# Moving the first part of a memory update from slot 8 to slot 9 of each segment's plan

## The chip, the cores and the metric

The kernel runs on one core of a Trainium2 chip. The metric is the device time of one execution in microseconds; less is better. TensorE (PE) multiplies, VectorE (DVE) and ScalarE (ACT) take results out of PSUM and do elementwise work, GpSimd (POOL) masks and adds in SBUF, SyncE (SP) issues nearly all DMAs.

## The reference

One layer over 2048 rows of width 640 in bf16. The rows are normalised and go through an attention with a compressive memory (32 heads of 20, 4 segments of 512 rows) and, separately, through a gated unit of width 1536; the output joins the two.

```python
xn = _layernorm(x)
for s in range(N):                      # 4 segments of L = 512
    p = softmax(einsum('bhqd,bhkd->bhqk', qs, ks) * scale + mask)
    a_dot = einsum('bhqk,bhkd->bhqd', p, vs)
    a_mem = einsum(phi(qs), M) / (einsum(phi(qs), z) + 1e-06)
    o = g * a_mem + (1.0 - g) * a_dot
    M = M + einsum('bhld,bhle->bhde', phi(ks), vs)
    z = z + einsum('bhld->bhd', phi(ks))
s = o @ wo
out = x + s * silu((sigmoid(xn @ w_gate) * (xn @ w_up)) @ w_down)
```

Here `phi(t)` is `t + 1` where `t > 0` and `exp(t)` elsewhere. The memory `M, z` that segment n leaves is read in segment n + 1.

## The kernel before

Every engine's work is issued in an order written out by the program; each engine runs its own queue in that order, and a wait holds what stands behind it. A segment is 20 slots (`NSLOT`), one pass over the heads in 4 pairs of head groups, five slots `u` = 0 to 4 for each pair (`UNITS`). A head group is 4 heads.

In a slot (the loop from L716) the program issues in this order:

- `scores` (L516): score matmuls `Sps` into four PSUM banks, of which there is one set only; then the exponential `pt` on ScalarE (L527, 128x2048) and the causal select on GpSimd (L530). The next slot's scores need the exponential done.
- an early part: tasks of the plan due before `now + 0.45`, and filler.
- `weigh` (L534) of the slot before: matmuls `Aps` of `pt` with the values, into a PSUM bank of which there is one. A head group ends with `u` = 2 for the first group and `u` = 4 for the second; then VectorE makes rd, rd and od (L553, L554, L556), and od frees that bank. The weighting of slot `u` runs in slot `u + 1`, so a head group ends in slots whose place in the pair is 3 (slots 3, 8, 13, 18) and 0.
- a late part: tasks due before `now + 1.0`, and filler.

All other matmuls write into a ring of three PSUM banks (`dtile`, tag "d"). Which of the three a new tile gets follows from the order in which earlier tiles were released in the program, so it is not strictly the oldest; TensorE then waits for the engine that reads that bank out. In the early part (`delay[0]`) k and v results are taken out by VectorE, otherwise by ScalarE.

The tasks have a due time in slots and a cost (`at`, L103). For the following segment: v tiles (`psv`, L360), k and q chunks (`psk` L289, `psq` L321), the q bound (`cps`, L334, copied out as `cb` and relayed through DRAM into QT); for the segment before: the o-projection (`sp`, L502, out as `aa`) and the output; for the segment itself the memory read (`mem_read`: matmuls `am` L410, then rm L415, rm L417 and om L418 on VectorE, om freeing the bank) and the memory update.

The memory update, `m_update` (L381), is issued in two parts: chunks 0 to 2 and chunks 3 and 4 of the 640 rows of `M`. The first part is 12 matmuls `dm` (L388) into one bank of the ring, then three VectorE products with a block mask. In segment 0 these write `Mbd` (L396). In segments 1 and 2 they write `dmb` (L399), of which there are two buffers, and GpSimd adds each into `Mbd` (L400). Segment 3 has none.

The filler is the gated unit: `gate` (`gp`, L428, five matmuls, then tg on ScalarE), `up` (L438, five matmuls, then hT on VectorE) and `down` (`yp`, L456, twelve matmuls). Before each segment the planner adds up what each slot already has, `fixed`, from a table of the weighting and the costs of the tasks due in it, and finds a common `level`; each slot's share of filler is what it lacks of that level. Shares add up in `goal`, and a filler group is issued when at least half its cost is covered:

```python
        fixed = [PASS[i % NU] + sum(t[2] for t in tasks if i <= t[0] - NSLOT * n < i + 1) for i in range(NSLOT)]
        level = min(fixed)
        while sum(max(level - f, 0.0) for f in fixed) < left:
            level += 0.01
```

Of the kernel before, what the change touches and what calls it, by code (L numbers as in the profile page):

```python
# [55 lines left out]
R = NSLOT / 24  # L56
# [3 lines left out]
def kernel(  # L60
# [42 lines left out]
    def at(time, cost, fn, *a):  # L103
        count[0] += 1
        heapq.heappush(first if fn is phi else tasks if cost > 0.1 else soft, (time, count[0], cost, fn, a))
# [533 lines left out]
    for n in range(NSEG):  # L639
        w = NSLOT * n  # L640
        m = n + 1
        if m < NSEG:
            if n:
                for p in range(2):
                    for i in range(2):
                        at(w + (-1.4, -0.7, 0.1, 0.55)[2 * p + i], 0.1, ln_stats, m, p, i, i + 1)
                        at(w + (0.6, 0.9, 1.7, 2.0)[2 * p + i], 0.1, ln_norm, m, p, i)
            for i in range(8):
                at(w + R * (3.5 + (0.6 * i if i < 4 else 2.5 + 0.55 * (i - 4))), 0.68, v_tile, m, i // 2, i % 2)
            for c in range(DC):  # L650
                at(w + R * (8.8 + 1.0 * c if n else 9.4 + 0.9 * c), 1.08, k_chunk, m, c)
                at(w + R * (13.8 + 1.1 * c), 1.08, q_chunk, m, c)
                if m + 1 < NSEG:
                    at(w + R * (12.8 + 0.85 * c), 0.0, phi, m, "k5", c)
                at(w + R * (17.4 + 0.8 * c), 0.0, phi, m, "q5", c)
            at(w + R * 19.2, 0.6, q_bound, m)
            if m + 1 < NSEG:
                for p in range(2):
                    at(w + R * (16.1 + p), 0.0, x_load, m + 1, p)
            if n == 0:  # L660
                for c in range(DC):
                    at(R * (2.6 + 0.8 * c), 0.0, phi, 0, "k5", c)
            for i, cs in enumerate(([0, 1, 2], [3, 4])):
                at(w + R * (10.0 + 3.2 * i), 0.75 - 0.25 * i, m_update, n, cs)
        if n >= 1:
            for j in range(4):
                at(w + R * (1.1 + 0.3 * j), 0.0, o_ready, n - 1, j)
                at(w + R * (4.0 + 0.5 * j if j < 3 else 9.6), 0.0, xr_load, n - 1, j)
            for i in range(8):
                at(w + R * (5.4 + 1.1 * i), 0.68, o_proj, n - 1, i // 2, i % 2)  # L670
                at(w + R * (3.4 + 0.85 * i), 0.25, mem_read, n, i // 2, i % 2)
# [74 lines left out]
    n = NSEG - 1  # L746
# [39 lines left out]
```

## Time and profile before

| | us |
|---|---|
| median of 3 runs | 338.39 |
| lowest, highest run | 338.29, 341.84 |
| profiled execution, its own time | 339.99 |
| its span, first to last instruction | 338.3 |

The page names an instruction group by line, engine and operation, with the tiles it writes and reads (out<-in). A row of the timeline has start, length, engine, line, operation, tiles, shapes and count; brackets at its end hold the engine's idle time just before it and the instruction whose end released it. A row of the chain of waits has start, length and the engine and tile on which the time depended. A row of waits has the total in us, the number of waits and the longest. Slots begin at the `Sps` rows: slot 8 of segment 0 at 60.53 us, of segment 1 at 134.23, of segment 2 at 213.47.

### The profile page before, as it was taken

To read this page: it belongs to the slowest core of one execution; us is meant where nothing else is said; L and a number is where in the kernel's file an instruction comes from. 1 tells how busy PE (TensorE), PEld (TensorE's weight loads), DVE (VectorE), ACT (ScalarE), POOL (GpSimd) and SP (SyncE) were. 2 spreads that over 40 slices of the span, in tenths; PEclk is the share of its full clock that TensorE was granted. 3 is DMA by queue.
4 is the path that set the end of the run, shared out by engine and by line. 5 is a ranking of instruction groups with operands and counts; after the bars stand their busy time and mean duration, and the time that the engine had idled before them with its cause. 6 is when DMAs were issued, how large, how long until landed. Compare 5 with 4: busy or idle time off the path is not lost.

```text
span 338.3 us, 8318 instructions
## 1 busy us (share of the span) xinstructions
PE 326.1 (96%) x3360; PEld 186.5 (55%) x3402; DVE 223.9 (66%) x532; ACT 226.5 (67%) x237; POOL 111.0 (33%) x157
## 2 busy tenths in 40 slices
PE   8999899999999999999999999999999999999995
PEld 7544455445665565554566466554456655544673
DVE  6375356479877577778775977876673687533355
ACT  3653797778786666477876765565887776786730
POOL 6645232232325322332223622333222323233214
PEclk9999999999999999999999999999999999999999
DMA  7956994774840731045730263042220521210032
GB/s 237 343 183 194 265 112 83 234 214 91 186 109 3 131 92 53 20 137 88 203 94 2 54 105 98 21 155 86 74 70 3 83 76 41 63 55 3 2 62 78
DMA packets 54725, 35.53 MB, mean 105 GB/s; under 512 B 28576, under 2 KB 54688, under 8 KB 54688
## 3 DMA queue, kind: packets, MB, share of 16 engines
q1 hardware_dynamic: 52480, 32.23, 37.7%
q10 hardware_dynamic: 2208, 2.79, 2.7%
q8 instruction: 26, 0.43, 0.6%
q14 instruction: 11, 0.09, 0.1%
HBM read 20.19 MB, written 8.39 MB: 84 GB/s over the span
## 4 chain that ended last, share of the span: by engine, by line
PE 87%; DMA 5%; DVE 3%; ACT 2%; issue 1%; POOL 0%; SPq 0%; DVEq 0%; ACTq 0%; POOLq 0%
PE yp L456 14%; PE up L438 14%; PE gp L428 13%; PE Aps L547 9%; PE Sps L522 7%; PE sp L502 6%; PE psk L289 6%; PE psq L321 6%; PE psv L360 6%; DMA Wu<-in_B_w_up_dram 2%; PE wps L571 2%; DMA xnT<-xn 1%; PE dm L388 1%; PE am L410 1%; ACT pt L527 1%
## 5 line engine op out<-in xcount | busy, mean ns | idle before, releaser
L527 ACT ACTIVATE pt<-Sps 128x2048 bf16<-128x2048 f32 x80 | 150.1, 1876 | 24.6 <-PE Sps L522 21.3
L530 POOL TENSOR_SCALAR_AFFINE_SELECT pt<-pt 128x1024 bf16<-128x1024 bf16 (+1 forms) x80 | 76.4, 956 | 197.8 <-ACT pt L527 197.8
L438 PE MATMUL up<-xnT,Wu 128*128 128x512 bf16 x229 | 58.8, 379 | 1.5 <-DVE Mbd L396 0.7
L428 PE MATMUL gp<-xnT,Wg 128*128 128x512 bf16 x221 | 58.0, 379 | 2.1 <-DMA Wg<-in_B_w_gate_dram 0.9
L456 PE MATMUL yp<-Wd,hT 128*128 128x320 bf16 x384 | 57.1, 299 | 0.0
L442 DVE SCALAR_TENSOR_TENSOR hT<-tg,up 128x512 bf16<-128x512 bf16 x48 | 32.7, 681 | 32.1 <-PE up L438 29.2
L431 ACT ACTIVATE tg<-gp 128x512 bf16<-128x512 f32 x48 | 28.6, 597 | 35.4 <-PE gp L428 34.7
L547 PEld LDWEIGHTS <-pt 128*128 128x128 bf16 x1280 | 43.1, 96 | 14.7 <-DVE od L556 2.1
L547 PE MATMUL Aps<-va,pt 128*128 128x21 bf16 x1280 | 44.5, 173 | 0.9 <-DVE od L556 0.8
L456 PEld LDWEIGHTS <-hT 128*128 128x128 bf16 x384 | 35.4, 97 | 15.7 <-issue 2.8
L438 PEld LDWEIGHTS <-Wu 128*128 128x128 bf16 x240 | 21.4, 97 | 24.4 <-issue 3.1
L428 PEld LDWEIGHTS <-Wg 128*128 128x128 bf16 x240 | 20.9, 97 | 22.6 <-issue 1.7
L461 DVE SCALAR_TENSOR_TENSOR aa<-t,yp 128x320 bf16<-128x320 bf16 x32 | 15.4, 482 | 26.7 <-ACT t L459 26.5
L522 PE MATMUL Sps<-QT,KT 24*128 24x128 bf16 (+3 forms) x512 | 32.0, 301 | 0.8 <-ACT pt L527 0.4
L360 PE MATMUL psv<-Wv,xnT 128*128 128x320 bf16 x160 | 26.4, 299 | 0.2
L459 ACT ACTIVATE t<-yp 128x320 bf16<-128x320 f32 x32 | 14.0, 437 | 18.4 <-PE yp L456 17.2
L502 PE MATMUL sp<-Wo,oT 128*128 128x320 bf16 x160 | 25.9, 300 | 0.0
L321 PE MATMUL psq<-xnT,Wq 128*128 128x512 bf16 x96 | 23.6, 380 | 0.6 <-issue 0.5
L289 PE MATMUL psk<-xnT,Wk 128*128 128x512 bf16 x92 | 23.5, 379 | 0.5 <-issue 0.2
L522 PEld LDWEIGHTS <-KT 24*128 24x128 bf16 x512 | 9.3, 92 | 25.5 <-issue 23.9
L504 DVE SCALAR_TENSOR_TENSOR aa<-aa,sp 128x320 bf16<-128x320 bf16 x32 | 15.5, 484 | 9.5 <-PE sp L502 9.5
L502 PEld LDWEIGHTS <-oT 128*128 128x128 bf16 x160 | 14.5, 98 | 8.0 <-issue 2.0
(74 smaller groups left out, 327.3 us busy)
## 6 DMA issues: line engine op xcount, KB each, us to landing
KT<-Ks SPq DMA_DIRECT2D x32, 80.0 KB
QT<-Qs SPq DMA_DIRECT2D x32, 80.0 KB
xr<-in_A_x_dram SPq DMA_DIRECT2D x15, 160.0 KB
out_dram<-xr SPq DMA_DIRECT2D x15, 160.0 KB
xt<-in_A_x_dram SPq DMA_DIRECT2D x6, 320.0 KB
Wg<-in_B_w_gate_dram SPq DMA_DIRECT2D x3, 640.0 KB
Wu<-in_B_w_up_dram SPq DMA_DIRECT2D x3, 640.0 KB
Wd<-in_B_w_down_dram ACTq DMA_DIRECT2D x1, 1920.0 KB
```

The lines of the kernel that those rows point to most:

```text
L289: nc.tensor.matmul(ps[:], lhsT=W["k"][:, k, c * P:(c + 1) * P], rhs=s["xnT"][:, k, :], start=(k == 0), stop=(k == DC - 1))
L321: nc.tensor.matmul(ps[:], lhsT=W["q"][:, k, c * P:(c + 1) * P], rhs=s["xnT"][:, k, :], start=(k == 0), stop=(k == DC - 1))
L360: nc.tensor.matmul(ps[:], lhsT=s["xnT"][:, k, j * P:(j + 1) * P], rhs=W["v"][:, k, half * HB:(half + 1) * HB], start=(k == 0), stop=(k == ...
L428: nc.tensor.matmul(gp[:], lhsT=Wg[f // 4][:, k, fo:fo + P], rhs=s["xnT"][:, k, :], start=(k == 0), stop=(k == DC - 1))
L438: nc.tensor.matmul(ps[:], lhsT=Wu[f // 4][:, k, fo:fo + P], rhs=s["xnT"][:, k, :], start=(k == 0), stop=(k == DC - 1))
L442: empty(lambda: nc.vector.scalar_tensor_tensor(out=h[:], in0=tg[:], scalar=1.0, in1=ps[:], op0=ALU.add, op1=ALU.mult))
L456: nc.tensor.matmul(yp[:], lhsT=s["hT"][f][:, j * P:(j + 1) * P], rhs=W["d"][:, f, hs], start=(f == 0), stop=(f == FC - 1))
L502: nc.tensor.matmul(sp[:], lhsT=s["oT"][:, j, c, :], rhs=W["o"][:, c, hs], start=(c == 0), stop=(c == DC - 1))
L522: nc.tensor.matmul(Sps[:, r, c0:c0 + ncol], lhsT=kt[32 * r:32 * r + KR, gi, kb * P:(kb + 1) * P], rhs=qt[32 * r:32 * r + KR, gi, kb * P:L] ...
L527: nc.scalar.activation(pt[:], Sps[:], ACT.Exp, scale=SCALE)
L530: nc.gpsimd.affine_select(out=diag, in_=diag, compare_op=ALU.is_ge, fill=0.0, base=0, pattern=[[0, 4], [0, cnt], [1, P]], channel_multipli ...
L547: nc.tensor.matmul(A[:, qb, r, :], lhsT=pt[:, r, off:off + P], rhs=V[4 * (n % 2) + kb][:, 4 * g + r, :], start=first, stop=True, skip_grou ...
```

## The change

The first part's due time becomes 9.05 slots in every segment instead of `R * 10.0`, which is 8.33 with `R` = 20/24. The second part keeps 11.0. Costs stay 0.75 and 0.5. At 8.33 the first part falls into the early part of slot 8 (place 3 of its pair), at 9.05 into that of slot 9 (place 4). In segments 1 and 2 it then stands behind the k chunk due at 9.0; in segment 0 ahead of the one due at 9.33. As its cost leaves one slot of `fixed` for the next, the planner's shares change too.

```diff
-                at(w + R * (10.0 + 3.2 * i), 0.75 - 0.25 * i, m_update, n, cs)
+                at(w + (9.05, 11.0)[i], 0.75 - 0.25 * i, m_update, n, cs)
```

## The prediction

> **What bounds the kernel now.** I read the page's busy shares and its chain of waits first, then TensorE's waits, then the timeline around the moved step in each of the three segments that have it.
>
> ```profile
> span 338.3 us, 8318 instructions
> ...
> PE 326.1 (96%) x3360; PEld 186.5 (55%) x3402; DVE 223.9 (66%) x532; ACT 226.5 (67%) x237; POOL 111.0 (33%) x157
> ...
> PEclk9999999999999999999999999999999999999999
> ...
> PE 87%; DMA 5%; DVE 3%; ACT 2%; issue 1%; POOL 0%; SPq 0%; DVEq 0%; ACTq 0%; POOLq 0%
> ```
> TensorE is busy 326.1 of 338.3 us at its full clock and makes 87% of the chain. The same matmuls run after the change, so only TensorE's idle time can go or come. It has names:
>
> ```profile
> PE Aps L547 <- DVE od L556: 0.8, 2, 0.4
> PE up L438 <- DVE Mbd L396: 0.7, 1, 0.7
> ...
> PE Sps L522 <- ACT pt L527: 0.4, 1, 0.4
> ```
> The 0.7 and half of the 0.8 lie at the moved step. In segment 0, slot 8:
>
> ```profile
> 60.53 0.39 PE L522 MATMUL Sps<-QT,KT 24*128 24x512 bf16 x4
> ...
> 60.85 0.98 PE L388 MATMUL dm<-va,pkt 128*128 128x147 bf16 x12
> 61.67 0.35 PE L547 MATMUL Aps<-va,pt 128*128 128x21 bf16 x8
> ...
> 61.87 0.77 DVE L396 TENSOR_TENSOR Mbd<-dm,BD 128x147 bf16<-128x147 f32 x3 [3.48 <-PE dm L388]
> ...
> 62.69 1.24 PE L438 MATMUL up<-xnT,Wu 128*128 128x512 bf16 x5 [0.67 <-DVE Mbd L396]
> ```
> The `up` group was given the PSUM bank that dm had just used, so it waits until VectorE's three products are out: 0.67 us. In segment 1 the chain of waits itself leaves TensorE at this place:
>
> ```profile
> 137.57 0.82 PE dm L388 x12
> ...
> 138.41 0.33 DVE dmb L399
> ...
> 138.81 0.48 POOL Mbd L400
> ...
> 139.31 0.33 DVE dmb L399
> ...
> 140.65 0.50 DVE od L556
> ...
> 141.19 0.76 PE Aps L547 x24
> ```
> ```profile
> 141.19 0.76 PE L547 MATMUL Aps<-va,pt 128*128 128x21 bf16 x24 [0.43 <-DVE od L556]
> ```
> dm's three products, the third of them held by GpSimd's add (two dmb buffers), stand on VectorE ahead of the pass that ends the head group; od empties the only Aps bank late, and slot 9's 24 weighting matmuls idle 0.43 us. Segment 2 has the same order, but its `Aps` row carries no idle time:
>
> ```profile
> 219.85 0.75 PE L547 MATMUL Aps<-va,pt 128*128 128x21 bf16 x24
> ```
>
> **What the change removes.** The dm group (12 matmuls with their weight loads, no DMA) starts after slot 9's scores instead of slot 8's, so slot 8's rd, rd and od no longer have the products before them. Slot 9 ends no head group. In segment 0 the built order gives slot 8 `up`, Aps, `gate`, k and slot 9 dm, k, Aps x24; in segments 1 and 2 slot 9 is k, dm, o-projection, Aps x24, k. No `up` follows dm into its bank. Removed: 0.67 + 0.43 + 0 = 1.10 us.
>
> What is late next at these places: in segment 0, slot 9 loses a `gate` group and becomes the shortest stretch that an exponential must fit into.
>
> ```profile
> 64.94 0.40 PE L522 MATMUL Sps<-QT,KT 24*128 24x128 bf16 x8
> ...
> 65.53 1.88 ACT L527 ACTIVATE pt<-Sps 128x2048 bf16<-128x2048 f32 x1
> ...
> 66.36 0.75 PE L547 MATMUL Aps<-va,pt 128*128 128x21 bf16 x24
> ...
> 66.97 1.24 PE L428 MATMUL gp<-xnT,Wg 128*128 128x512 bf16 x5
> ...
> 68.14 0.40 PE L522 MATMUL Sps<-QT,KT 24*128 24x512 bf16 x4
> ```
> From the scores' start T, dm follows after 0.32 (60.53 to 60.85), takes 0.82 (60.85 to 61.67), a five-matmul group 1.17 (66.97 to 68.14), Aps 0.61 (66.36 to 66.97): the next scores at T + 2.92. The exponential ends at T + 0.59 + 1.88 = T + 2.47. It hides with 0.45 us over; cost nothing, and up to 0.4 if ScalarE is that late.
>
> **What the change adds.** Moving 0.75 of planned cost from one slot to another changes the planner's shares, and filler groups jump slots. In segment 0 only slots 8 and 9 change. In segment 1 a `gate` group leaves the end of slot 6 for slot 7, behind that slot's first memory read, another goes from slot 9 to slot 8, and a `down` group from slot 16 into slot 15. In segment 2 `gate` groups go from slot 3 to 4 and from 6 to 7, and an `up` from 12 to 11. Segment 3 keeps its order. Two of these groups were a cover:
>
> ```profile
> 130.13 1.24 PE L428 MATMUL gp<-xnT,Wg 128*128 128x512 bf16 x5
> ...
> 130.47 0.49 DVE L418 TENSOR_TENSOR om<-am,rm 128x320 bf16<-128x320 f32 x1
> ...
> 131.30 0.40 PE L522 MATMUL Sps<-QT,KT 24*128 24x256 bf16 x8
> ...
> 131.63 0.34 PE L410 MATMUL am<-Mbd,q 128*128 128x147 bf16 x3
> ...
> 131.80 0.84 PE L502 MATMUL sp<-Wo,oT 128*128 128x320 bf16 x5
> ```
> ```profile
> 209.36 1.24 PE L428 MATMUL gp<-xnT,Wg 128*128 128x512 bf16 x5
> ...
> 209.71 0.49 DVE L418 TENSOR_TENSOR om<-am,rm 128x320 bf16<-128x320 f32 x1
> ```
> While `gate` ran, VectorE finished om, which frees a bank. Without it the scores start where `gate` did, at 130.13, am at 130.46 (131.30 to 131.63 is 0.33), and the next group 0.17 later (131.63 to 131.80), at 130.63. In the built order that next group is the moved `gate` in segment 1, the o-projection in segment 2, and each is given the bank that om has to leave. om ends at 130.47 + 0.49 = 130.96: a wait of 0.33. In segment 2: 209.36 + 0.50 = 209.86 against 210.20, 0.34. Behind that group on TensorE's queue stand the slot's k group and weighting, so it is lost in full; VectorE, which it waits for, is late whatever TensorE does. Bounds for each: 0, if Aps and scores take up more of the time than I count, and 0.45, if the scores start 0.1 earlier than `gate` did, an allowance. I take 0.33, as the rows are of the same instructions. Together 0.67 us. The third move of this shape, segment 2's slot 3 to 4, finds its bank free just about in time by the same count; I put it at nothing, with 0.3 as its other end.
>
> The moved step is also put behind slot 9's select on GpSimd's queue in segments 1 and 2. No DMA moves past another on SyncE's queue; stage-out of k waits for the k copy, which now stands ahead of the products on VectorE, so nothing queues behind them there.
>
> **The sum.** 1.10 removed, 0.67 added: 0.43 us less. The profiled execution took 339.99 us, 1.7 outside its span; it would become 339.56. The median of the runs shown is 338.39, 1.60 below the profiled one; the same subtraction gives 337.96, so 338.0 us. One percent, 3.4 us, is about what a measurement of this kernel can tell from no change.
>
> **Rivals.** First, the new waits do not come: VectorE and TensorE shift together and only the removal counts, 338.39 - 1.10 = 337.3. For it: the bank waits rest on 0.3 us. Against: om's chain on VectorE starts at a product that does not move earlier.
>
> Second, and on the other side, GpSimd. In the changed segments 1 and 2 its queue has slot 9's select first, then the three adds; VectorE's third product waits for the first add, and the slot-10 o-projection waits for that product's bank, with the aa product and the residual add queued behind it on VectorE.
>
> ```profile
> 138.50 0.40 PE L522 MATMUL Sps<-QT,KT 24*128 24x128 bf16 x8
> ...
> 139.01 1.88 ACT L527 ACTIVATE pt<-Sps 128x2048 bf16<-128x2048 f32 x1 [2.40 <-PE Sps L522]
> ...
> 140.96 1.10 POOL L530 TENSOR_SCALAR_AFFINE_SELECT pt<-pt 128x1024 bf16<-128x1024 bf16 x1 [0.67 <-ACT pt L527]
> ```
> From T = 138.50: the select ends at 142.06, T + 3.56; add 0.48 and product 0.33 and a few hundredths, T + 4.4. TensorE reaches that o-projection after the scores 0.33, k 1.17, dm 0.82, o-projection about 0.68 (an estimate between Aps 0.61 and dm 0.82), Aps 0.61, k 1.17, scores 0.33: T + 5.1. It decides once GpSimd is over 0.7 us later than this.
>
> ```profile
> L554 DVE TENSOR_TENSOR rd<-rd,omg x32: 174/175/666, 47.1 to 324.4; 128x16 f32<-128x16 f32 x32
> ```
> The same small product takes 0.175 us at the median and 0.666 once, so something holds an engine up to 0.49 us; that leaves 0.2 of the margin. The Trainium skill (SBUF — State Buffer, "SBUF: two separate sides") has a rule for this: VectorE with two SBUF inputs and GpSimd take one shared port pair as an exclusive lock for a whole instruction, and the loser blocks. By it the sum stays 0.43 less if one such hold falls on the adds, and this rival decides if two do; the row's spread agrees with it, though it does not show which engine held.
>
> If it decides, the price lies between 0.3 and, with one more select of 1.10 in the way, 1.1 us in each of two segments: 337.96 + 0.6 = 338.6 up to 340.2; typically 339.0, slower than before.
>
> Third, the tail of segment 1. With `down` ahead of it, slot 16 holds the bound's group, Aps and one `down` alone, as segment 0's slot 16 does already, and there TensorE waited later:
>
> ```profile
> 95.65 0.40 PE L522 MATMUL Sps<-QT,KT 24*128 24x512 bf16 x4 [0.41 <-ACT pt L527]
> ```
> If ScalarE's copies and exponentials pile up alike, 0.41 more: 338.4, no change. Against it: the planner leaves the order of ScalarE's work there nearly alone. The bound's copy cb comes one `down` group, 1.74 us, later, and goes by DRAM to the next segment's first scores; no matmul of before waited for that relay:
>
> ```profile
> 168.08 1.74 PE yp L456 x12
> ...
> 173.53 2.88 SPq L353 DMA_DIRECT2D QT<-Cs  x8
> ...
> 184.08 0.39 PE L522 MATMUL Sps<-QT,KT 24*128 24x512 bf16 x4
> ```
> The last of its loads is issued by 176.41, 7.7 us ahead of those scores, which hides the shift unless a load needs over 5.9 us; nothing is counted.
>
> That the step stays where it was is no rival: the built order has it in slot 9.
>
> Fourth, the reordered filler opens waits that I did not follow, several of 0.3 to 0.7 us or a long one: over 3.4 us would need ten like those found, so 342 or more.
>
> **How the numbers follow.** Forecast 0.55 (337.96 within 0.3), first rival 0.15, second 0.13, third 0.07, fourth 0.06; 0.04 is left for a gain that no row explains. The forecast and the first three rivals lie within one percent, 0.90 in all, of which 0.03 is given up to a median as high as the highest run shown, 341.84. That makes faster 0.04, within one percent 0.87 and slower 0.06 + 0.03 = 0.09. The range runs from the first rival less 0.6 of spread, 336.7, to the second's upper part, 339.8; it leaves out the fourth and the unexplained gain.
>
> **What would show it.** TensorE's wait of `up` for Mbd gone; its waits of Aps for od once, not twice; new waits of about 0.3 for om before `gate` in segment 1's slot 7 and before the o-projection in segment 2's slot 7. Without those, the first rival. A wait of the o-projection for dmb shows the second, of the scores for pt in segment 1 the third. It is wrong if TensorE's named idle changes by over 1 us, or the time moves while that idle does not.

## The result and the profile after

The changed kernel took 337.88 us (median of 22 runs, 336.94 to 339.14), the kernel before 338.40 beside it (22 runs, 337.20 to 341.99). The ratio is 0.9968, 95% interval 0.9954 to 0.9983: a little faster, by 0.6 to 1.6 us, well within the one percent. Here and below the ratio is not the quotient of the two medians, which lie only 0.52 us apart; the means, 337.86 and 338.91, lie 1.05 apart. The forecast was 338.0.

The profiled execution went from a span of 338.3 to 335.6 us. That is 2.7 less, more than the ratio allows, so the two profiles must also differ in things that the change didn't touch. The page of the changed kernel:

```profile
span 335.6 us, 8361 instructions
...
PE 328.0 (98%) x3402; PEld 186.1 (55%) x3402; DVE 224.0 (67%) x532; ACT 226.1 (67%) x237; POOL 111.6 (33%) x157
...
PE 86%; DMA 6%; DVE 3%; ACT 2%; SPq 1%; issue 1%; DVEq 0%
```

TensorE still bounds it. Its busy time appears to grow from 326.1 to 328.0, but the records grow with it (x3360 to x3402 of the same 3402 weight loads): some matmul records are missing from the trace of before. The view of TensorE's waits (us in total, times, longest) is the better guide:

```profile
PE wps L571 <- POOL ident L180: 1.4, 1, 1.4
PE pT L260 <- DVE xn L253: 0.3, 1, 0.3
PE gp L428 <- DVE om L418: 0.3, 1, 0.3
PE up L438 <- DMA Wu<-in_B_w_up_dram: 0.3, 1, 0.3
PE sp L502 <- DVE om L418: 0.3, 1, 0.3
PE psv L360 <- DMA xnT<-xn: 0.3, 1, 0.3
```

Gone are `up` for Mbd, Aps for od (both of its two waits), the scores for pt, and the wait for the gate weights' transfer (0.9 before). New are two of 0.3 for om. To see where the time went, the table takes the starts of the score groups (`Sps`) in each trace and shows how long each stretch of slots took. Outside segment 0's first and last slots, the stretches of one order repeat to 0.02 us from one execution to the next, so these lengths can be read far more closely than the times of whole runs.

| slots | before | before again | after | after again | step alone | filler alone | segment 0 alone | segments 1, 2 alone | best of both | second select |
|---|---|---|---|---|---|---|---|---|---|---|
| start to segment 0, slot 8 | 60.53 | 60.07 | 59.58 | 59.74 | 59.28 | 59.99 | 60.74 | 59.63 | 59.51 | 60.00 |
| segment 0, 8 to 10 | 10.61 | 10.61 | 9.78 | 9.78 | 9.97 | 11.23 | 9.79 | 10.60 | 9.79 | 9.78 |
| segment 0, 16 to 19 | 14.64 | 13.68 | 13.67 | 13.68 | 14.23 | 13.67 | 14.38 | 13.68 | 13.68 | 13.68 |
| segment 1, 6 and 7 | 7.63 | 7.64 | 7.94 | 7.94 | 7.64 | 7.93 | 7.64 | 7.93 | 7.63 | 7.93 |
| segment 1, 8 and 9 | 9.83 | 9.83 | 9.23 | 9.24 | 9.23 | 9.24 | 9.83 | 9.24 | 9.23 | 9.24 |
| segment 1, 10 | 3.28 | 3.28 | 3.28 | 3.28 | 3.27 | 3.28 | 3.27 | 3.28 | 3.27 | 3.90 |
| segment 2, 6 and 7 | 7.63 | 7.64 | 7.94 | 7.94 | 7.62 | 7.94 | 7.62 | 7.94 | 7.62 | 7.93 |
| segment 2, 8 and 9 | 8.15 | 8.15 | 8.16 | 8.16 | 8.16 | 8.16 | 8.16 | 8.16 | 8.17 | 8.16 |
| segment 2, 10 | 3.28 | 3.28 | 3.28 | 3.28 | 3.28 | 3.27 | 3.28 | 3.28 | 3.27 | 3.90 |

From before to after: segment 0 is 0.83 shorter, segment 1 is 0.31 longer in slots 6 and 7 and 0.60 shorter in slots 8 and 9, segment 2 is 0.31 longer. That is 0.81 us less, inside the interval of 0.6 to 1.6. The other 1.9 us between the two profiles lie in the first row (0.95) and in segment 0's slots 16 to 19 (0.97), and these two differ between executions of one kernel too: the second profile of before has 60.07 and 13.68 there. They are not the change's.

Here is the timeline of TensorE in the changed kernel, first in segment 0 (slots 8 and 9), then in segments 1 and 2:

```profile
59.58 0.39 PE L522 MATMUL Sps<-QT,KT 24*128 24x512 bf16 x4
59.90 1.25 PE L438 MATMUL up<-xnT,Wu 128*128 128x512 bf16 x5
60.99 0.35 PE L547 MATMUL Aps<-va,pt 128*128 128x21 bf16 x8
61.20 1.24 PE L428 MATMUL gp<-xnT,Wg 128*128 128x512 bf16 x5
62.27 1.24 PE L289 MATMUL psk<-xnT,Wk 128*128 128x512 bf16 x5
63.45 0.40 PE L522 MATMUL Sps<-QT,KT 24*128 24x128 bf16 x8
63.78 0.98 PE L388 MATMUL dm<-va,pkt 128*128 128x147 bf16 x12
64.60 1.24 PE L289 MATMUL psk<-xnT,Wk 128*128 128x512 bf16 x5
65.68 0.75 PE L547 MATMUL Aps<-va,pt 128*128 128x21 bf16 x24
66.36 0.40 PE L522 MATMUL Sps<-QT,KT 24*128 24x512 bf16 x4
...
126.81 0.55 PE L547 MATMUL Aps<-va,pt 128*128 128x21 bf16 x16
127.30 0.40 PE L522 MATMUL Sps<-QT,KT 24*128 24x256 bf16 x8
127.63 0.34 PE L410 MATMUL am<-Mbd,q 128*128 128x147 bf16 x3
128.29 1.25 PE L428 MATMUL gp<-xnT,Wg 128*128 128x512 bf16 x5 [0.32 <-DVE om L418]
...
138.59 0.84 PE L502 MATMUL sp<-Wo,oT 128*128 128x320 bf16 x5
139.27 0.75 PE L547 MATMUL Aps<-va,pt 128*128 128x21 bf16 x24
...
141.37 0.85 PE L502 MATMUL sp<-Wo,oT 128*128 128x320 bf16 x5
...
207.26 0.85 PE L502 MATMUL sp<-Wo,oT 128*128 128x320 bf16 x5 [0.32 <-DVE om L418]
```

dm stands behind slot 9's scores and nothing waits for its products. Slot 9 of segment 0 is 66.36 - 63.45 = 2.91 us long. In segment 1 the 24 weighting matmuls follow the o-projection at 0.68, with no idle time. Two groups carry 0.32 of idle time for om.

### The profile page after: what moved, and what is told of

It reads as the page before. It is cut to its first block, busy times and chain, and to the rows that moved or that the text cites. A ratio compares the mean times of both kernels' runs of the same rounds, so it can differ in the third digit from the quotient of the medians.

```text
span 335.6 us, 8361 instructions
## 1 busy us (share of the span) xinstructions
PE 328.0 (98%) x3402; PEld 186.1 (55%) x3402; DVE 224.0 (67%) x532; ACT 226.1 (67%) x237; POOL 111.6 (33%) x157
## 4 chain that ended last, share of the span: by engine, by line
PE 86%; DMA 6%; DVE 3%; ACT 2%; SPq 1%; issue 1%; DVEq 0%
PE yp L456 15%; PE up L438 14%; PE gp L428 14%; PE Aps L547 9%; PE Sps L522 7%; PE sp L502 7%; PE psk L289 6%; PE psv L360 6%; PE psq L321 5%; DMA Wu<-in_B_w_up_dram 2%; DMA Ks<-k 2%; DMA xnT<-xn 1%; PE dm L388 1%; ACT pt L527 1%; PE am L410 1%; DMA Qs<-q 1%
## 5 line engine op out<-in xcount | busy, mean ns | idle before, releaser
L428 PE MATMUL gp<-xnT,Wg 128*128 128x512 bf16 x240 | 59.6, 379 | 0.4 <-DVE om L418 0.3
L438 PE MATMUL up<-xnT,Wu 128*128 128x512 bf16 x240 | 59.7, 379 | 0.3 <-DMA Wu<-in_B_w_up_dram 0.3
L321 PE MATMUL psq<-xnT,Wq 128*128 128x512 bf16 x100 | 24.3, 380 | 0.0
L289 PE MATMUL psk<-xnT,Wk 128*128 128x512 bf16 x100 | 24.2, 379 | 0.0
```

Of the source, the lines that this page charges most:

```text
L289: nc.tensor.matmul(ps[:], lhsT=W["k"][:, k, c * P:(c + 1) * P], rhs=s["xnT"][:, k, :], start=(k == 0), stop=(k == DC - 1))
L321: nc.tensor.matmul(ps[:], lhsT=W["q"][:, k, c * P:(c + 1) * P], rhs=s["xnT"][:, k, :], start=(k == 0), stop=(k == DC - 1))
L428: nc.tensor.matmul(gp[:], lhsT=Wg[f // 4][:, k, fo:fo + P], rhs=s["xnT"][:, k, :], start=(k == 0), stop=(k == DC - 1))
L438: nc.tensor.matmul(ps[:], lhsT=Wu[f // 4][:, k, fo:fo + P], rhs=s["xnT"][:, k, :], start=(k == 0), stop=(k == DC - 1))
```

## The experiments

All of them were timed beside the kernel before, the first four on one chip and the last four on another. Before took 338.97 us on the first (median of 35 runs) and 338.59 on the second (35 runs).

**Both kernels again.** Two copies without an edit, to learn how far two executions of one kernel differ.

> The kernel before, unchanged, profiled a second time. Of the 2.7 us between the two profiled spans, the step theory explains the waits at the moved step (0.67 and 0.43 gone, two of 0.32 new); it expects the 0.67 and the 0.43 here again within 0.05. What it does not explain are 1.1 us ahead of slot 1 (the wait for the first gate weights, 0.90) and the waits at the ends of slots 17 and 19 of segment 0 (0.41 for pt, 0.40 for od). Theory A: these three belong to single executions (transfers landing earlier or later), and at least one of them is absent or differs by over 0.2 us here. Rival B: they belong to the order of before, and all three are here again within 0.1.

> The changed kernel, unchanged, profiled a second time. Step theory: the two waits for om of 0.32 again, no wait of up for Mbd, no wait of Aps for od in segment 1; ratio to before 0.996 to 0.999. Theory A on slots 17 and 19 of segment 0: the waits for pt and od may be here or not, as the transfers fall. Rival B: they are absent.

Measured: before again 338.91 us, ratio 1.0003 [0.9985, 1.0022]; after again 338.07, ratio 0.9971 [0.9954, 0.9989]. The difference repeats. In before again the waits of `up` for Mbd (0.7) and of Aps for od in segment 1 (0.4) are back; the scores' wait for pt and the second wait for od are absent, and the one for the gate weights is 0.3 instead of 0.9. So theory A holds for these three: they belong to the execution. In after again both waits for om are back.

**The step alone.** The first part moves to 9.05, but the planner counts its cost at the old place, so that the filler's shares stay those of before.

```diff
-                at(w + R * (10.0 + 3.2 * i), 0.75 - 0.25 * i, m_update, n, cs)
+                at(w + (9.05, 11.0)[i], 0.75 - 0.25 * i, m_update, n, cs)
...
-        fixed = [PASS[i % NU] + sum(t[2] for t in tasks if i <= t[0] - NSLOT * n < i + 1) for i in range(NSLOT)]
+        def due_of(t):
+            if t[3] is m_update and t[4][1][0] == 0:
+                return NSLOT * t[4][0] + R * 10.0
+            return t[0]
+        fixed = [PASS[i % NU] + sum(t[2] for t in tasks if i <= due_of(t) - NSLOT * n < i + 1) for i in range(NSLOT)]
```

> The step alone: the first part runs at 9.05, but the planner counts its cost in slot 8 as before, so the filler keeps the slots of before. Step theory: both old waits gone, neither wait for om, so 1.10 us less than before: ratio 0.9968, and 0.67 us less than the changed kernel. Rival: the gain of the change comes from the new places of the filler; then this kernel is no faster than before, ratio 1.000.

Measured: 337.27 us, ratio 0.9955 [0.9936, 0.9974]. By the table, 0.64 less in segment 0 and 0.60 less in segment 1, no new wait: 1.24 less. The interval shuts out the rival's 1.000. The 1.10 expected is short by 0.14, since it is the prediction's sum of two idle times (see the next section). So the 0.62 in slots 6 and 7 of segments 1 and 2 are the filler's, not the step's. In segment 0 this order gains 0.19 less than the changed kernel's, so by the table it lies 0.43 under that kernel and not the 0.67 expected. The place of the difference is seen in the timeline of its slot 8:

```profile
59.28 0.39 PE L522 MATMUL Sps<-QT,KT 24*128 24x512 bf16 x4
59.61 0.54 PE L547 MATMUL Aps<-va,pt 128*128 128x21 bf16 x8
60.00 1.24 PE L438 MATMUL up<-xnT,Wu 128*128 128x512 bf16 x5
```

Directly behind the scores the eight weighting matmuls take 60.00 - 59.61 = 0.39 us from start to start; behind `up`, in the changed kernel, they take 61.20 - 60.99 = 0.21. The difference, 0.18, is what segment 0 lacks here; why the place behind the scores costs more stays open.

**The filler alone.** The reverse: the step stays at 8.33 and the planner counts its cost at 9.05.

```diff
-        fixed = [PASS[i % NU] + sum(t[2] for t in tasks if i <= t[0] - NSLOT * n < i + 1) for i in range(NSLOT)]
+        def due_of(t):
+            if t[3] is m_update and t[4][1][0] == 0:
+                return NSLOT * t[4][0] + 9.05
+            return t[0]
+        fixed = [PASS[i % NU] + sum(t[2] for t in tasks if i <= due_of(t) - NSLOT * n < i + 1) for i in range(NSLOT)]
```

> The filler alone: the first part runs at 8.33 as before, but the planner counts its cost in slot 9, so the filler stands as in the changed kernel. Step theory: two waits for om of 0.32; in segment 0 the up group follows dm at once, so its wait for Mbd grows from 0.67 to about 1.0; in segment 1 a gate group stands before slot 9, which covers od, so the 0.43 goes. Together 0.65 + 0.33 - 0.43 = 0.55 us more than before: ratio 1.0016. Rival (the filler brings the gain): ratio 0.997.

Measured: 339.20 us, ratio 1.0019 [1.0002, 1.0036]: slower by 0.64 by the ratio, though the interval only just shuts out no change and the medians lie 0.23 apart. The rival's 0.997 is out. By the table: 0.62 more in segment 0, 0.59 less in segment 1's slots 8 and 9, 0.30 and 0.31 more in the two pairs of slots 6 and 7, together 0.64 more. Its timeline in segment 0:

```profile
60.32 0.98 PE L388 MATMUL dm<-va,pkt 128*128 128x147 bf16 x12
62.16 1.24 PE L438 MATMUL up<-xnT,Wu 128*128 128x512 bf16 x5 [0.86 <-DVE Mbd L396]
...
68.22 0.40 PE L522 MATMUL Sps<-QT,KT 24*128 24x512 bf16 x4 [0.35 <-ACT pt L527]
```

Here `up` directly follows dm into its bank and waits longer than before, as expected: dm takes 0.82 to the next group's start, so `up` starts 62.16 - 61.14 = 1.02 late, against 0.81 before. With the `gate` group gone to slot 8 but dm not come to slot 9, the exponential is no longer covered, which was not expected: the scores wait for pt, 0.43 counted from the 0.68 that the same pair of groups takes in the changed kernel. Slot 9 now lasts 68.22 - 65.70 = 2.52 us. The wait of segment 1's slot 9 goes with the filler alone as well: it goes when dm leaves slot 8 (the step alone), and it also goes when a `gate` group stands between the two weightings and gives VectorE some 1.1 us more to empty the Aps bank. Either one is enough; the other then brings nothing.

**Segment 0 alone, segments 1 and 2 alone.** The step at 9.05 in some segments only, the planner counting it where it is.

```diff
-                at(w + R * (10.0 + 3.2 * i), 0.75 - 0.25 * i, m_update, n, cs)
+                at(w + ((R * 10.0, 9.05)[n == 0], 11.0)[i], 0.75 - 0.25 * i, m_update, n, cs)
```

and `n > 0` in the place of `n == 0`.

> Only segment 0 has the first part at 9.05; segments 1 to 3 are in the order of before. By the stretches of the changed kernel, slots 8 to 10 of segment 0 take 9.78 us instead of 10.61: 0.83 less, ratio about 0.9976, all other slots as before. By the prediction's term, the wait of 0.67 as the trace counts it, 0.67 less and slots 8 to 10 at 9.94. If the gain of segment 0 were of another place (the start or its last slots, which differ from execution to execution), ratio 1.000.

> Only segments 1 and 2 have it at 9.05; segment 0 keeps the order of before, with its wait of up for Mbd of about 0.7. By the stretches: segment 1 slots 8 and 9 0.60 less, slots 6 and 7 0.31 more; segment 2 slots 6 and 7 0.31 more; sum 0.02 more, ratio 1.000. By the prediction's terms 0.43 less and 0.67 more, sum 0.24 more, ratio 1.0007. If the new waits cost nothing net, 0.6 less, ratio 0.998.

Measured: segment 0 alone 337.70 us, ratio 0.9978 [0.9962, 0.9995]; segments 1 and 2 alone 338.42, ratio 0.9995 [0.9979, 1.0012]. The table has 0.82 less for the first: slots 8 to 10 take 9.79 and not the 9.94 of the idle time 0.67. For the second it has 0.59 less and 0.30 and 0.31 more, which cancel. The times alone would not tell this from 0.6 less or 0.24 more, as the interval holds both; the table does. So the net gain is segment 0's. In segments 1 and 2 the filler gives back what the step brings.

**Best of both.** The step at 9.05 in all three segments; the planner counts it there in segment 0 and at the old 8.33 in segments 1 and 2. It is the step alone with one more condition:

```diff
-            if t[3] is m_update and t[4][1][0] == 0:
+            if t[3] is m_update and t[4][1][0] == 0 and t[4][0] > 0:
```

> The first part at 9.05 in all three segments; the planner counts its cost there in segment 0, and at the old 8.33 in segments 1 and 2, so that no filler moves in these. By the stretches 0.83 + 0.60 = 1.43 less, ratio about 0.9958, no wait for om and none of up for Mbd; 0.19 under the kernel with the planner as before in all segments, which is too little to be told from it by the times alone and is to be read in slots 8 to 10 of segment 0 (9.78 against 9.97). If the parts do not add up, no faster than the changed kernel, 0.997.

Measured: 337.30 us, ratio 0.9961 [0.9945, 0.9977], span 334.9. By the table 0.82 + 0.60 = 1.42 less, as expected. By the times it can't be told from the step alone, nor, as the intervals overlap, from the changed kernel. Its waits of TensorE, the same view as above:

```profile
PE wps L571 <- POOL ident L180: 1.4, 1, 1.4
PE pT L260 <- DVE xn L253: 0.5, 2, 0.3
PE psq L321 <- issue: 0.5, 3, 0.2
PE psv L360 <- DMA xnT<-xn: 0.4, 1, 0.4
PE up L438 <- DMA Wu<-in_B_w_up_dram: 0.3, 1, 0.3
PE gp L428 <- issue: 0.2, 1, 0.2
```

No wait for Mbd, om, od or pt is left. What remains is the start, with DMAs and the first transposes (three of these six lines), the one wait for `ident`, and two lines of "issue", time in which the profile shows nothing that TensorE waited for.

**A second select.** The changed kernel, with slot 9's select issued twice on GpSimd in segments 1 and 2. It tests the second rival: whether a late GpSimd decides, and from which point.

```diff
+        if n in (1, 2) and pair == 1 and u == 4:
+            nc.gpsimd.affine_select(out=diag, in_=diag, compare_op=ALU.is_ge, fill=0.0, base=0,
+                                    pattern=[[0, 4], [0, cnt], [1, P]], channel_multiplier=-1)
         return pt
```

> The changed kernel with slot 9's select issued twice on GpSimd in segments 1 and 2 (the second time it changes nothing), 1.10 us of GpSimd each, ahead of the adds. If the second rival's mechanism is right and decides from the margin in the changed kernel's trace (third product ends at T + 4.44, o-projection starts at T + 5.01), the third product ends at about T + 5.54 and slot 10's o-projection waits about 0.5 in each of the two segments for dmb: 1.0 to 1.3 more than the changed kernel, ratio to before about 1.000 to 1.001. If GpSimd has slack there, no such wait, and ratio 0.997 as the changed kernel.

Measured: 339.10 us, ratio 1.0016 [1.0002, 1.0030], a little above the 1.000 to 1.001 expected; slot 10 takes 3.90 instead of 3.28 in both segments, 1.24 more in all, as expected (1.0 to 1.3). From the waits of TensorE:

```profile
PE sp L502 <- DVE dmb L399: 1.1, 2, 0.6
```

and from its timeline in segment 1, on TensorE, VectorE and GpSimd:

```profile
136.78 0.40 PE L522 MATMUL Sps<-QT,KT 24*128 24x128 bf16 x8
...
142.44 0.84 PE L502 MATMUL sp<-Wo,oT 128*128 128x320 bf16 x5 [0.57 <-DVE dmb L399]
...
142.05 0.33 DVE L399 TENSOR_TENSOR dmb<-dm,BD 128x168 bf16<-128x168 f32 x1 [2.31 <-POOL Mbd L400]
...
139.32 1.10 POOL L530 TENSOR_SCALAR_AFFINE_SELECT pt<-pt 128x1024 bf16<-128x1024 bf16 x1 [3.96 <-ACT pt L527]
140.49 1.10 POOL L533 TENSOR_SCALAR_AFFINE_SELECT pt<-pt 128x1024 bf16<-128x1024 bf16 x1
141.55 1.48 POOL L400 TENSOR_TENSOR Mbd<-Mbd,dmb 128x147 bf16<-128x147 bf16 x3
```

The mechanism is there. With T = 136.78 the third product ends at 142.38, T + 5.60, and the o-projection starts right behind it at T + 5.66. In the changed kernel, from its GpSimd and VectorE timelines, the same product ends 4.44 after the scores' start of 136.36, and the o-projection starts at 141.37, 5.01 after it:

```profile
138.90 1.10 POOL L530 TENSOR_SCALAR_AFFINE_SELECT pt<-pt 128x1024 bf16<-128x1024 bf16 x1 [3.96 <-ACT pt L527]
...
140.47 0.33 DVE L399 TENSOR_TENSOR dmb<-dm,BD 128x168 bf16<-128x168 f32 x1 [1.14 <-POOL Mbd L400]
```

So the margin is 0.57 us, and of a delay of 1.16 (T + 4.44 to T + 5.60) it took 0.57; TensorE lost the rest, 0.59 by this count and 0.62 by the slot's length.

## Why the prediction was nearly right

**What was right.** No change by one percent, and a gain by the mechanism named. The two new waits came at the places forecast, `gate` in segment 1's slot 7 and the o-projection in segment 2's, and cost 0.31 each in the table, against 0.33 and 0.34. The exponential's cover in segment 0's slot 9 was forecast with 0.45 to spare, and no wait for pt appeared; against the 2.52 of the filler alone, where pt sets the slot's length, the spare time is 2.91 - 2.52 = 0.39. Segment 2's slots 3 and 4 took 7.12 before and 7.13 after, and no wait for the relayed bound appeared, as put down.

**What was luck.** The median, 337.88 against 338.0, is closer than the account behind it: the forecast gain was 0.43, and the table shows 0.81. The 0.33 for om holds because two errors cancel, as the rows of segment 1 show. The wait itself is 0.49 by starts: `gate` starts 128.29 - 127.63 = 0.66 behind am, where the next group follows at 0.17 without a wait (131.63 to 131.80 before). The scores start 0.49 behind the 16 weighting matmuls and not 0.59, as `gate` had, which is the 0.1 that the prediction allowed for in its upper bound, and `gate` starts 0.06 after om's end. Against that the `gate` group costs TensorE 1.09 in its new slot and 1.27 in its old one, by the starts around it, which gives 0.18 back. The length of segment 0's slot 9 (2.91 against 2.92) is also made up of two errors: k up to Aps takes 1.08 and not 1.17, Aps up to the scores 0.68 and not 0.61.

**The step that was off** is the size of the removed terms: 0.67 + 0.43 in "What the change removes". In the table they were worth 0.83 and 0.60. The idle time in a row's brackets is counted from the modelled end of the matmuls before it, and TensorE starts the next group before that end where it doesn't have to wait (in the changed kernel the o-projection's modelled end is 138.59 + 0.84 = 139.43, and Aps starts at 139.27). In segment 1 this row of before's timeline stands ahead of the Aps at 141.19:

```profile
139.92 0.84 PE L502 MATMUL sp<-Wo,oT 128*128 128x320 bf16 x5
```

Its modelled end is 140.76, 0.43 ahead of Aps. But up to the start of Aps the group takes only 0.68 in the changed kernel (138.59 to 139.27). Without the wait Aps would have started at 140.60, not 141.19: 0.59 lost, not 0.43. Segment 0: eight weighting matmuls take 0.21 up to the next group, so `up` would have started at 61.67 + 0.21 = 61.88 instead of 62.69: 0.81, not 0.67. The prediction had the right method and used it for the slot lengths, but took the bracketed idle for the price of a wait. With these two terms, and 0.62 for the two moved groups by the table, the sum is 0.81 + 0.59 - 0.62 = 0.78 less, against 0.43. The interval of the first comparison, 0.6 to 1.6, excludes 0.43; that of the second (0.9954 to 0.9989, or 0.4 to 1.6 us of 338.97) holds 0.43 and 0.8.

**A reading that was wrong** is that segment 2 had the same order as segment 1 around its Aps of slot 9. There `up` stood behind the eight weighting matmuls, and in segment 1 ahead of dm:

```profile
216.58 1.24 PE L438 MATMUL up<-xnT,Wu 128*128 128x512 bf16 x4
```

So in segment 2 TensorE had another group to do while VectorE emptied the Aps bank, and VectorE took out `up` (hT, 0.59 in segment 1's chain of waits) after od and not before it. od ended 1.25 us after slot 9's scores there, and 2.64 after them in segment 1. The zero in the sum was right, but dm's products alone were not enough to make the wait; the filler alone shows the same for `gate`.

**The expectation for Aps and od**, one wait left of two, was off: none was left, and the step alone has one again. The second belongs to segment 0's slots 16 to 19 and to the execution, not the kernel (last section). The 0.41 of scores for pt, on which the third rival rested, lies in the same four slots and went with it; so that rival's row was no sign of what its kind of slot costs. Segment 1's slots 15 to 17 took 11.72 us before and 11.73 after. The prediction's sign of being wrong, idle with a name changed by over 1 us, did come: the lines of the view, without "issue", add up to 4.4 us before and 2.9 after. But in the second pair of profiles they are 3.5 and 3.2, so that sign does not tell the change from what executions differ by.

**The rivals.** The first (only the removal counts) is out as the prediction put it: the new waits came. Its number, 1.1 us less, is near to what the means show (1.05), but by another sum, which is chance. The second did not decide: the margin was 0.57 where 0.7 was counted, and in the changed kernel nothing used it up. That it decides once GpSimd is later than that, slower than before, is shown by the second select. For the fourth no sign is left: the view of TensorE's waits after holds no names but the six shown.

**The share of the planner.** The prediction gave the whole change one sum. The experiments divide it: the step alone 1.24 less, the filler's new shares in segments 1 and 2 0.62 more, and segment 0's new order 0.19 less beside the step.

## What to carry to other kernels

The price of a wait is the distance from one group's start to the next, less the same distance where the pair doesn't wait; the idle time in the row is short of it, here by 0.14 to 0.17 us of 0.5 to 0.8. What a moved group costs in all is read from whole stretches, since the groups around its old and its new place change their distances too: here 0.31 for a wait of 0.49. A step that a planner schedules has two effects, its own move and that of all it pushes about: try the one without the other before keeping both, since here the second gave back half of what the first brought. Margins of half a microsecond, read off the trace of before, held in the changed kernel, though 0.06 and 0.13 smaller than counted, and adding work to the engine behind one is a cheap way to learn what it covers.

## What the runs showed of the hardware

Two things moved the profiles by as much as the change. The start differed by up to 1.5 us (59.28 to 60.74 us up to slot 8). And segment 0's slots 16 to 19 took 13.67 or 13.68 us in seven of ten profiled executions and 14.23, 14.38 and 14.64 in the other three, one of which is the profile of before. In these three alone VectorE waited for a DMA (Qs<-q) ahead of its products for q, and then one VectorE instruction beside GpSimd's select took more than twice its time. The step alone, on VectorE, GpSimd, ScalarE and TensorE:

```profile
87.97 0.29 DVE L373 TENSOR_SCALAR q<-q 128x512 bf16<-128x512 bf16 x1 [0.22 <-DMA Qs<-q]
...
89.23 1.61 DVE L374 SCALAR_TENSOR_TENSOR q<-ex,q 128x512 bf16<-128x512 bf16 x1
...
89.19 1.10 POOL L530 TENSOR_SCALAR_AFFINE_SELECT pt<-pt 128x1024 bf16<-128x1024 bf16 x1 [3.43 <-ACT pt L527]
...
90.93 0.63 ACT L370 ACTIVATE ex<-q 128x512 bf16<-128x512 bf16 x1 [0.91 <-DVE q L374]
...
98.07 0.76 PE L547 MATMUL Aps<-va,pt 128*128 128x21 bf16 x24 [0.40 <-DVE od L556]
```

The changed kernel, VectorE and GpSimd, at the same place and, in the last two rows, in slot 8:

```profile
89.18 0.69 DVE L374 SCALAR_TENSOR_TENSOR q<-ex,q 128x512 bf16<-128x512 bf16 x1
...
89.30 1.53 POOL L530 TENSOR_SCALAR_AFFINE_SELECT pt<-pt 128x1024 bf16<-128x1024 bf16 x1 [3.43 <-ACT pt L527]
...
62.15 0.67 DVE L554 TENSOR_TENSOR rd<-rd,omg 128x16 f32<-128x16 f32 x1
...
62.11 0.68 POOL L530 TENSOR_SCALAR_AFFINE_SELECT pt<-pt 128x512 bf16<-128x512 bf16 x1 [1.99 <-ACT pt L527]
```

In these rows whichever starts first keeps its usual length, 0.69, 1.10 or 0.68, and the other one is long: the product 1.61 where the select began 0.04 earlier, the select 1.53 where the product began 0.12 earlier, the small product of slot 8 0.67 for 0.175 where the select began 0.04 earlier. The loser ends 0.55, 0.96 and 0.03 after the winner, in all three cases 0.14 short of its own usual length: but for that, the two run one after the other. The same holds for slot 17's select in the other traces: in nine of the ten a VectorE instruction on q was running when the select began, and the select ended 0.96 after that instruction, with lengths of 1.16 to 1.60; in the step alone it kept its 1.10. This agrees with the Trainium skill (SBUF — State Buffer, "SBUF: two separate sides"), by which the two engines' shared port pair is a lock that the first one holds for a whole instruction; the prediction left open which engine holds the other, and these rows show both cases. When the product loses, ScalarE's `ex` waits 0.91 for it, its queue runs late, and two slots later TensorE waits for od. Counted from slot 17's scores (89.18 and 89.28), the product began 0.05 after them in the one and 0.10 before them in the other: 0.15 us, with a DMA that landed late ahead of it, goes with 0.55 us of the execution. In the profile of before, where another instruction of VectorE lost (L373, 1.19 for 0.28), it is 0.96. That is argued from the traces of ten executions; no kernel was run that sets the order of the two by hand.
